# TensorE's waits on itself behind the borders of its instruction pieces: further back and more of them

## The chip, the cores and the metric

The kernel runs on one core of one Trainium2 chip. The metric is the device time of one launch in microseconds. Five engines of the core work side by side, each with its own instruction stream: TensorE (PE, with its weight loads PEld), VectorE (DVE), ScalarE (ACT), GpSimd (POOL) and SyncE (SP), which here issues the transfers. They wait for each other by semaphores.

## What is computed

The input x has 2048 tokens of 512 values. It is normalized, and an attention with a memory runs over it in 64 segments of 32 tokens; each segment's 8 memory rows come out of the segment before, so the segments form a chain. A two-layer network with gelu follows for all tokens.

```python
# A: for each of 64 segments, M = 8 memory rows, 32 heads of 128
h = concatenate([mem, xs]);  q, k, v = h @ Wq, h @ Wk, h @ Wv
p = softmax(mask(q k^T * 128**-0.5));  o = (p v) @ Wo
mem = o[:, :8];  outs.append(o[:, 8:])
# whole
h  = x + A(layernorm(x))
h2 = h + gelu(layernorm(layernorm(h)) @ w1 + b1) @ w2 + b2     # 512 -> 1792 -> 512
```

## The kernel before

All weights of the attention stay in SBUF (WQ, WK, WV, WO). A segment multiplies a pack hT of 32 columns (24 tokens and 8 memory rows) with WQ, WK and WV. A matmul with 32 stationary columns fills a quarter of the array, so four of them, on four column groups, run together: four matmuls of 512 columns are one *unit* of a projection. The remaining 8 tokens of each of four segments are gathered in a second pack, hB, and projected once per four segments; this work (called F in the program) fills places where TensorE would wait. Then come the scores of memory rows (SC0, SC1: L1122) and of tokens (SA: L1179), two softmaxes on VectorE, ScalarE and GpSimd, the products with v (PV0, PV1, PVA: L1153, L1157, L1225, L1231) and the output projection (WO: L1264, a run of 64 matmuls of 256 columns in eight units; L1303 for hB). L946 are matmuls that load their weights, L689 matmuls that reuse those that the array holds, L944 weight loads without a matmul. The last stage, behind some 710 us, is the two-layer network (L1660, L1667).

The program is recorded as a list of operations with estimated durations, and a scheduler (class `Sched`) writes each engine's stream from it. TensorE's order is fixed by hand; each operation gets a planned start, and from the planned order the scheduler works out which semaphore each operation must wait for. An operation signals its engine's semaphore on its last instruction only if somebody waits for it.

TensorE's stream is some 40,000 instructions. The program takes it to come in pieces of 256 instructions (`FETCH_N`). The method `pads` inserts harmless extra weight loads (L944) to move the borders of the pieces to chosen places, `windows` keeps transfers off the times of the borders, and `pauses` is the one that this change touches:

```python
for first in self.heads:                       # first unit behind each border
    n, i = 0, first
    while n < PAUSES and i < len(pe) and pe[i].at < pe[first].at + PAUSE_IN:
        o = pe[i]
        j = bisect.bisect_right(ends, o.start - PAUSE_US) - 1
        if not o.waits and 0 <= j < i:
            o.waits = [pe[j]]
            pe[j].sig = True
            n += 1
        i += 1
```

A unit close behind a border that waits for nothing else gets a wait on the last unit of TensorE itself that by plan ended at least `PAUSE_US` before it. TensorE executes in order, so such a wait orders nothing: it holds back the reading of instructions until the array has got so far. The numbers are at L31.

Of the kernel before, what the change touches and what calls it, by code (L numbers as in the profile page):

```python
# [27 lines left out]
LATE = dict(Q0=0.1, K0=0.1, Q1=-0.5, K1=-0.4, V0=2.0, SC0=2.0, SC1=1.6, V1=1.8, F=1.3, PV0=1.0, PVA=1.0, PV1=0.95, WO=0.4, F2=0.5, SA=0.5)  # L28
KEEP = True
WINDOWS, WIN_LO, WIN_HI, WIN_BEHIND = True, 1.0, -0.8, 0.4  # L30
PAUSES, PAUSE_IN, PAUSE_US = 3, 64, 0.5  # L31
KEPT, LEAD = 3, 9
REST = (0, 1, 4, 5, 6, 8, 9)
ORDER0 = (6, 7, 8, 9, 10, 11, 0, 1, 2, 3, 4, 5, 12, 13)
# [1746 lines left out]
```

## Time and profile before

| what | us |
|---|---|
| median of 3 runs | 805.2 (802.64 to 805.48) |
| the profiled execution, its time | 805.6 |
| its span, first to last instruction | 803.9 |
| TensorE busy | 770.4 |
| VectorE, ScalarE, GpSimd busy | 585.3, 529.2, 311.4 |
| the stage of the segments | about 60 to 700 |

A segment takes a little over 10 us there: the runs of L1264, one per segment, start at 223.18 and 233.81 us, for instance. The rows name a line, an engine, an operation and the tiles as out<-in; "x" is a count; "idle before" is the time that the engine stood still before it, with what ended it. A weight load has its own row (PEld) and runs beside matmuls. The ends of matmuls are modelled, so the steps from start to start tell more than the lengths.

### The profile page before, as it was taken

How to read it: one execution, taken by the hardware profiler on the slowest of the kernel's cores; microseconds unless marked ns; L12 is line 12 of the kernel's file. 1: busy time of each engine (PE TensorE's matmuls, PEld its weight loads, DVE VectorE, ACT ScalarE, POOL GpSimd, SP SyncE). 2: the span in 40 equal slices, each digit the busy share in tenths (PEclk: the TensorE clock that was granted, in tenths of full speed). 3: DMA queues.
4: the chain of work that ended last, by engine and by line, in shares of the span. 5: the costliest groups of instructions: out<-in, count | busy, mean ns of one | idle time of the engine just before them, and what ended most of it. 6: DMA issues, size and time to landing. Idle time of an engine off the chain costs nothing.

```text
span 803.9 us, 44855 instructions
## 1 busy us (share of the span) xinstructions
PE 770.4 (96%) x19573; PEld 423.6 (53%) x20093; DVE 585.3 (73%) x1865; ACT 529.2 (66%) x1381; POOL 311.4 (39%) x836
## 2 busy tenths in 40 slices
PE   4788999999999999999999999999999999999998
PEld 1345455555555555556665555556556564544443
DVE  3267888888888888888888888888888887833111
ACT  1446777767776777776767777777776777653342
POOL 3013223444343444444434444444453425276200
PEclk9989999999999999999999999999999999999999
DMA  8960000111201010103020201030112222266200
GB/s 337 393 194 11 3 21 20 24 38 23 37 15 46 10 50 10 44 11 57 4 52 8 52 9 50 11 50 4 50 31 62 45 58 53 62 184 157 53 27 26
DMA packets 65453, 48.11 MB, mean 60 GB/s; under 512 B 29028, under 2 KB 61676, under 8 KB 65260
## 3 DMA queue, kind: packets, MB, share of 16 engines
q1 hardware_dynamic: 64928, 44.98, 20.4%
q8 instruction: 156, 2.56, 1.4%
q14 instruction: 37, 0.30, 0.1%
q10 hardware_dynamic: 332, 0.27, 0.1%
HBM read 31.08 MB, written 8.13 MB: 49 GB/s over the span
## 4 chain that ended last, share of the span: by engine, by line
PE 91%; DMA 2%; DVE 2%; SPq 2%; issue 1%; ACT 1%; DVEq 0%
PE high L946 33%; PE high L689 17%; PE quad L1264 15%; PE quad L1667 6%; PE high L1660 5%; PE high L1303 3%; DMA WQ<-in_A_Wq_dram 2%; SPq L849 2%; PE quad L1122 2%; PE quad L1179 2%; PE quad L1225 2%; PE high L1459 2%; PE high L1153 1%; PE quad L1153 1%; PE high L1264 1%
## 5 line engine op out<-in xcount | busy, mean ns | idle before, releaser
L946 PE MATMUL high<-WQ,hT 128*32 128x512 bf16 x1796 | 158.2, 383 | 3.8 <-DVE hT L1270 3.0
L1202 POOL TENSOR_TENSOR PA<-SA,rsa 128x256 bf16<-128x256 f32 x64 | 39.6, 619 | 235.5 <-DVE rsa L1194 148.0
L689 PE MATMUL high<-WK,hT 128*32 128x512 bf16 x1260 | 127.3, 379 | 0.1
L1264 PE MATMUL quad<-WO,OT 128*32 128x256 bf16 x4032 | 122.7, 273 | 0.2 <-issue 0.2
L946 PE MATMUL high<-WV,hT 128*32 128x512 bf16 x1528 | 117.0, 381 | 0.0
L965 ACT ACTIVATE kq<-high 128x512 bf16<-128x512 f32 x160 | 94.2, 598 | 26.7 <-PE high L946 23.3
L964 ACT CAST kq<-high 128x512 bf16<-128x512 f32 x161 | 93.7, 582 | 21.4 <-PE high L946 19.6
L1264 PEld LDWEIGHTS quad<-WO,OT 128*32 128x32 bf16 x4032 | 101.9, 97 | 6.9 <-issue 1.7
L1210 POOL COPY BD<-PTA 32x128 f32<-32x128 f32 x256 | 79.6, 311 | 16.3 <-DVE PTA L1206 0.6
L946 PEld LDWEIGHTS high<-WQ,hT 128*32 128x32 bf16 x1796 | 52.8, 95 | 62.0 <-issue 28.9
L987 DVE STREAM_TRANSPOSE KALL<-kq 128x256 f32<-128x256 f32 x160 | 69.4, 434 | 10.9 <-ACT kq L964 8.1
L964 ACT CAST VS<-high 128x512 bf16<-128x512 f32 x126 | 73.1, 580 | 0.0
L944 PEld LDWEIGHTS <-hT 128*32 128x32 bf16 x3064 | 50.7, 96 | 32.7 <-DVE hT L1270 6.3
L1276 DVE STREAM_TRANSPOSE TT<-quad 128x256 f32<-128x256 f32 x63 | 28.3, 449 | 50.8 <-PE quad L1264 50.7
L1663 ACT ACTIVATE WQ<-high,b1t 128x512 bf16<-128x512 f32 x42 | 28.9, 687 | 51.9 <-PE high L1660 51.9
L964 ACT CAST OT<-quad 128x128 bf16<-128x128 f32 (+1 forms) x128 | 47.8, 375 | 21.8 <-PE quad L1157 21.5
L1021 ACT COPY KALL<-KALL 128x128 f32<-128x128 f32 x62 | 18.5, 298 | 59.0 <-PE quad L1179 58.8
L987 DVE STREAM_TRANSPOSE QT<-kq 128x256 f32<-128x256 f32 x128 | 54.8, 428 | 1.9 <-ACT kq L965 1.6
L946 PE MATMUL high<-WK,hT 128*32 128x512 bf16 x788 | 55.4, 379 | 0.0
L1122 PEld LDWEIGHTS quad<-KALL,ZC 128*32 128x32 bf16 x2016 | 32.3, 96 | 42.2 <-POOL BD L1210 18.1
L689 PE MATMUL high<-WV,hT 128*32 128x512 bf16 x520 | 54.5, 387 | 0.0
L1316 POOL TENSOR_TENSOR opT<-TTB,TTS 32x64 bf16<-32x64 f32 x128 | 40.0, 312 | 35.0 <-DVE opT L1270 18.6
(182 smaller groups left out, 1612.4 us busy)
## 6 DMA issues: line engine op xcount, KB each, us to landing
WV<-in_A_Wv_dram SPq DMA_DIRECT2D x4, 1024.0 KB, 10.5
WK<-in_A_Wk_dram SPq DMA_DIRECT2D x4, 1024.0 KB, 18.5
WQ<-in_A_Wq_dram SPq DMA_DIRECT2D x4, 1024.0 KB, 20.4
WO<-in_A_Wo_dram SPq DMA_DIRECT2D x16, 256.0 KB, 7.6
v_last<-VSB SPq DMA_DIRECT2D x60, 64.0 KB, 2.2
VBD<-v_last SPq DMA_DIRECT2D x60, 64.0 KB, 2.6
h_mid<-xr SPq DMA_DIRECT2D x16, 128.0 KB, 2.0
WQ<-h_mid SPq DMA_DIRECT2D x4, 512.0 KB, 4.2
```

What stands on the lines that cost most here:

```text
L689: return e.add_instruction(mybir.InstMatmult(name="I-%d" % (4000000 + _kept[0]), engine=mybir.EngineType.PE, start_tensor_calc=start, stop ...
L944: e.ldweights(l, tile_position=(0, 32 * j))
L946: ins = e.matmul(o, l, m, start=(k == 0), stop=(k == DC - 1), tile_position=(0, 32 * j), skip_group_check=True)
L964: return {"act": (lambda e: e.copy(out, src), t_act(n, ps_)), "dve": (lambda e: e.tensor_copy(out, src), 0.155 + 1.0e-3 * n * fast)}
L965: return {"act": (lambda e: e.mul(out, src, scale_), t_act(n, ps_)), "dve": (lambda e: e.tensor_scalar(out, src, scale_, None, ALU.mult), ...
L987: S.op("dve", lambda e: e.transpose(out, src), reads=[("kq", i)], writes=[key], dur=t_dve(256) + 0.02)
L1122: ins = e.matmul(o[32 * j:32 * j + 32, :], zc_window(h), rhs, start=False, stop=(i == 3), tile_position=(0, 32 * j), skip_group_check=True)
L1210: S.narrow(S.op("pool", lambda e, j=j, rows=rows: e.tensor_copy(words(BD[rows, par, :, j, :, :]), words(PTA[rows, 0:4])), reads=["PTA"], w ...
L1264: ins = e.matmul(ps[bank][32 * j:32 * j + 32, 0:256], lhs(slot(h)), wo_cols(h, b), start=(k == 0), stop=(k == 15), tile_position=(0, 32 * ...
L1316: return e.tensor_tensor(o[32 * q:32 * q + 32, c:c + 2], x, y, ALU.add)
L1660: ins = e.matmul(ps[bank][:, 0:SBT], W1[:, cc, fc * P:(fc + 1) * P], hnT_of(k)[:, cc, :], start=(cc == 0), stop=(cc == DC - 1))
L1667: S.op("pe", lambda e: e.matmul(quad[:, t, :], gT_of(k, fc)[:, t * P:(t + 1) * P], W2[:, fc, :], start=(fc == (0 if k else ORDER0[0])), st ...
```

## The change

Three numbers: up to ten units behind a border get a wait, where it was three; they may lie up to 192 instructions behind the border's first unit, where it was 64; and the unit waited for has by plan ended 0.9 us ago, where it was 0.5.

```diff
-PAUSES, PAUSE_IN, PAUSE_US = 3, 64, 0.5
+PAUSES, PAUSE_IN, PAUSE_US = 10, 192, 0.9
```

No operation is added, moved or taken away on any engine: only waits and signals of TensorE on itself. Of the 407 waits of TensorE on itself, all stay, 394 of them on another unit than before; there are 1343 now. The signals on TensorE rise from 1270 to 1936.

The first place, on TensorE: the piece that begins at about 221.4 us in the trace. Its first wait (L946, group at 221.81) stays and points two units further back, which the order doesn't show. Behind it come the products with v, and then the run of L1264; sem_act is ScalarE's semaphore, sem_pe TensorE's own. The piece's end is in the run of L1179 behind it.

```order
 L1157 MATMUL high<-PTC,VBD 128x64 x2
 L1264 MATMUL quad<-WO,OT 32x256 [waits sem_act]
-L1264 MATMUL quad<-WO,OT 32x256 x31
-L1264 MATMUL quad<-WO,OT 32x256 [waits sem_act]
-L1264 MATMUL quad<-WO,OT 32x256 x31
+L1264 MATMUL quad<-WO,OT 32x256 x7
+L1264 MATMUL quad<-WO,OT 32x256 [waits sem_pe]
+L1264 MATMUL quad<-WO,OT 32x256 x7
+L1264 MATMUL quad<-WO,OT 32x256 [waits sem_pe]
+L1264 MATMUL quad<-WO,OT 32x256 x7
+L1264 MATMUL quad<-WO,OT 32x256 [waits sem_pe]
+L1264 MATMUL quad<-WO,OT 32x256 x7
```

Nothing moved; five new waits stand in this run (three shown, two more behind the second wait on ScalarE), between waits on ScalarE that were there.

The second place, on TensorE: the end of such a run, then hB's output projection and the token scores of another segment (at about 163 us), where a piece has fewer waits on other engines.

```order
 L1264 MATMUL quad<-WO,OT 32x256 [waits sem_act]
-L1264 MATMUL quad<-WO,OT 32x256 x31
-L1303 MATMUL high<-WO,OTB 32x512 x8
+L1264 MATMUL quad<-WO,OT 32x256 x7
+L1264 MATMUL quad<-WO,OT 32x256 [waits sem_pe]
+L1264 MATMUL quad<-WO,OT 32x256 x7
+L1264 MATMUL quad<-WO,OT 32x256 [waits sem_pe]
+L1264 MATMUL quad<-WO,OT 32x256 x7
+L1264 MATMUL quad<-WO,OT 32x256 [waits sem_pe]
+L1264 MATMUL quad<-WO,OT 32x256 x7
+L1303 MATMUL high<-WO,OTB 32x512 [waits sem_pe]
+L1303 MATMUL high<-WO,OTB 32x512 x3
```

Here, too, only waits came in, one for each unit.

## The prediction

> **What bounds the kernel now.** I read the page's busy times and clock first, then the middle stage by windows, then TensorE's waits in it, then the chain. The page:
>
> ```profile
> span 803.9 us, 44855 instructions
> PE 770.4 (96%) x19573; PEld 423.6 (53%) x20093; DVE 585.3 (73%) x1865; ACT 529.2 (66%) x1381; POOL 311.4 (39%) x836
> PEclk9989999999999999999999999999999999999999
> q8 instruction: 156, 2.56, 1.4%
> PE 91%; DMA 2%; DVE 2%; SPq 2%; issue 1%; ACT 1%; DVEq 0%
> ```
>
> TensorE is busy for 96% at full clock and is 91% of the chain. The q8 line is how its program arrives: 156 packets, 2.56 MB, so 16 KB each; 19573 matmuls and 20093 weight loads over 156 packets are about 255 instructions a packet. These are the pieces of the change. The stage of the segments (columns: us, then busy us and count of PE, PEld, DVE, ACT, POOL, clock, DMA share, GB/s) and TensorE's own waits in it (total, times, longest):
>
> ```profile
> 60.00:640.00 580.00, 572.85 (x16648) 329.05 (x17272) 487.95 (x1595) 423.11 (x1152) 245.29 (x680) 1.00 0.13 29
> PE quad L1179 <- issue: 2.1, 8, 0.4
> PE high L946 <- DVE hT L1270: 2.0, 3, 0.8
> PE high L1153 <- DVE PTC L1139: 0.8, 2, 0.5
> PE high L946 <- issue: 0.7, 3, 0.4
> PE quad L1153 <- ACT EC L1131: 0.3, 1, 0.3
> PE high L1157 <- issue: 0.3, 2, 0.2
> PE quad L1264 <- issue: 0.2, 1, 0.2
> ```
>
> In 580 us TensorE lacks 7.15 us of being busy all the time. The largest part of its waits is "issue", time in which no semaphore was late: 2.1 + 0.7 + 0.3 + 0.2 = 3.3 us in 14 stops. None of TensorE's rows names TensorE as releaser. One of the stops, in order of time:
>
> ```profile
> 224.76 0.28 PE L1264 MATMUL quad<-WO,OT 128*32 128x256 bf16 x4
> 225.08 0.39 PE L689 MATMUL high<-WQ,hB 128*32 128x512 bf16 x4
> 225.30 0.21 PE L1179 MATMUL quad<-KALL,QT 128*32 128x40 bf16 x7
> 225.83 0.34 PE L1179 MATMUL quad<-KALL,QT 128*32 128x40 bf16 x25 [0.32 <-issue]
> ```
>
> A run of 32 equal matmuls stops after the seventh. In the program the first of the 32 is instruction 242 of its piece, and seven matmuls with their weight loads are 14 instructions: the stop is at instruction 256, on the border. So I read "issue" here as a piece that came late. The transfers of that time (40 slices of 0.1 us from 222 to 226):
>
> ```profile
> GB/s 0 0 0 0 0 0 0 0 0 164 0 0 0 0 0 0 0 0 0 0 0 0 0 0 0 0 0 0 0 0 0 0 0 0 0 0 0 0 0 0
> q8 instruction: 1, 0.02, 2.0%
> ```
>
> One packet, nothing beside it: it starts at 222.9 and takes 2.0% of 16 engines over 4 us, 1.28 us, so it lands near 224.2, and the starved matmul starts 1.6 us later. The border before it lies in the group that starts at 221.38 (next fence), so the packet started 1.5 us behind that border. A faster start of that packet is the only thing that the change could win.
>
> **What the change does, part by part.** The built program has the same 40058 TensorE instructions in the same order, and the other queues are unchanged, SP's and POOL's too. Waits of TensorE on itself rise from 407 to 1343 and its signals from 1270 to 1936.
>
> *The 407 waits that stay* point further back: in projections at the unit six back, where it was four. The place just behind that border:
>
> ```profile
> 221.38 0.40 PE L946 MATMUL high<-WQ,hB 128*32 128x512 bf16 x4
> 221.59 0.40 PE L689 MATMUL high<-WQ,hB 128*32 128x512 bf16 x4
> 221.60 0.12 PEld L946 LDWEIGHTS high<-WQ,hB 128*32 128x32 bf16 x4 [0.32 <-PE high L946]
> 221.81 0.40 PE L946 MATMUL high<-WQ,hB 128*32 128x512 bf16 x4
> 222.03 0.40 PE L689 MATMUL high<-WQ,hB 128*32 128x512 bf16 x4
> ```
>
> The weight load at 221.60 waited 0.32 us on TensorE's own work, and the matmuls go on every 0.215 us without a gap: today's waits cost nothing. Their spare time: the unit four back starts 4 x 0.215 = 0.86 ahead and lasts 0.40, and the weights load 0.21 ahead, which leaves 0.25 us. Six back it is 1.29 - 0.40 - 0.21 = 0.68 us. What is queued behind such a wait is TensorE's own stream alone; the other engines wait for matmuls, which don't move. Term: 0.
>
> *The 936 new waits* have the same 0.68 us of spare time. Bound from rows of the chain:
>
> ```profile
> 213.09 1.86 PE quad L1264 x64
> 223.18 1.86 PE quad L1264 x64
> 510.89 1.95 PE quad L1264 x64
> 582.35 2.00 PE quad L1264 x64
> 634.60 2.04 PE quad L1264 x64
> ```
>
> The run of 64 at 213.09 has three such waits in it, the one at 223.18 none; both take 1.86. With a resolution of 0.01 us that is at most 0.01/3 = 3.3 ns a wait, 3.1 us for 936. Below: no reason for a gain in itself. I take 0, since the two rows are equal, and keep 3.1 as the upper end. (The three rows over 1.86 are runs with a border in them: small stops.)
>
> *The 666 new signals.* The same two runs have one signal more in the one than in the other, so at most 10 ns each, 6.7 us for all, if each lay bare. They end a group whose followers are already streaming, and the steps above don't change; I take 0. The Trainium skill has a rule that speaks against the change: in "TensorE: Matmul & The Clock Gate", section "The cost: per-tile semaphore tail", each increment on a matmul's end adds 26.3 ns to the tail, since increments are written one after another. An estimate by that page is 666 x 26.3 ns = 17.5 us, if no tail were covered; the equal runs of 1.86 don't show it.
>
> *What goes away as a hold.* At 221.60 the hold of 0.32 us is shorter than the 0.43 us by which the wait moves back, so it vanishes, and the sequencer gets past that place up to 0.32 us sooner. If the next piece is asked for when the sequencer has got so far, the packet at 222.9 moves forward. But next in its way stand waits on VectorE and ScalarE for the group L1153, which the change leaves alone. What is at stake: 14 stops of 3.3 us by the waits view, each longer by the modelled length of the matmul ahead of it,
>
> ```profile
> L1179 PE MATMUL quad<-KALL,QT 128*32 128x40 bf16 x2016 | 27.4, 182 | 2.4 <-issue 2.1
> ```
>
> so 3.3 + 14 x 0.18 = 5.8 us, and with small stops like 2.04 - 1.86 = 0.18 in the rows above about 7 us. That is the whole prize. Ends: -7 and 0 by this; I take a tenth, -0.7 us, nearest to no gain, since the VectorE wait takes the hold over.
>
> *What stands longer.* Up to ten waits reach to instruction 192 of a piece, where three reached to 64. They keep the sequencer within 0.68 us plus a weight load of the array over much of a piece, where it could run further ahead. A piece entered later asks for its successor later. In the run of L1264 (the first of the two places in the section on the change) the new waits stand between two waits on ScalarE that are there anyway, and near the next border there are again such waits. Term: 0, with an upper end of 0.3 us a stop, 14 x 0.3 = 4.2 us.
>
> The Trainium skill, "Runtime: NRT & Kernel Launch", section "Instruction fetch mechanics", says that programs stream in 16 KiB blocks of 256 instructions and that a border's cost is mostly hidden. The trace agrees with the size (16 KB, 255) and not quite with the rest: 14 of some 140 borders in this stage stop TensorE. By that rule the prize would be 0 and the time 805.2.
>
> **Sum.** 0 + 0 + 0 - 0.7 + 0 = -0.7 us against the profiled execution's 805.6 (span 803.9 and 1.7 around it): 804.9. That execution is 0.4 above the median 805.2, so the median comes to 804.5 us.
>
> **Rivals.**
>
> *Pieces come sooner.* The vanished hold (0.32 at 221.60) starts the packet sooner at most starved borders: 14 x 0.3 = 4.2 us, 801.0; at most 7, 798.2. For it: the hold stands right behind the border of the piece whose successor was late. Against: the waits on VectorE and ScalarE close behind.
>
> *Pieces come later* (the other side). The longer hold puts the sequencer 0.3 us later over the borders; the 14 starved pieces lose 14 x 0.3 = 4.2 us, 809.4, and pieces that now come just in time join them. It decides from about 0.3 us a piece on. For it: two rows show stops of 0.4 us already, so there is no reserve. Against: 64 units of L1264 take 1.86 us, with or without waits.
>
> *Signals cost.* 10 ns each, bare: +6.7, 811.9; a third of it would be 807.4. Against: the equal steps of 0.215 us.
>
> *Nothing changes at all.* The waits are all long satisfied and the packets start as before: 805.2. This and my forecast can't be told apart by time.
>
> **Chances.** The likeliest (804.5) and "nothing changes" together 0.70; pieces sooner 0.16; pieces later 0.10; signals 0.04. A change is told from none by about 0.5%, 4.0 us. So faster 0.17 (the sooner rival and a little of the spread of 802.64 to 805.48 in the runs), slower 0.12 (the later rival and the dearer half of the signals), same 0.71. The range for 8 in 10 reaches down to the sooner rival's 4.2 us, 801.0, and up to 804.5 + 3.1 (the bound of the waits), 807.6; outside lie about 0.08 below and 0.10 above.
>
> **What would show it.** If I am right: TensorE's waits on "issue" in this stage again 2 to 5 us in 10 to 20 stops, on borders; runs of L1264 at 1.86 us with five more waits in them; the projection step still 0.215 us; weight loads that wait on PE shorter than 0.32 each, though there are more of them. The sooner rival: issue rows nearly gone, packets of q8 earlier behind their borders. The later rival: more stops, longer, at the same places. Signals: runs of L1264 longer than 1.86 everywhere, by 0.01 or more a signal. I am wrong if the request of a piece depends on something the waits do to the sequencer that this trace can't show, since 0.2 us on each packet is worth about 3 us.

## The result and the profile after

The changed kernel takes 822.74 us (median of 4 runs, 820.94 to 826.45) against 803.99 us (4 runs, 802.64 to 805.48) for the kernel before, measured beside it: 1.0247 times as long, 95% interval 1.0223 to 1.027. It is slower by about 19 us, where I had forecast 804.5 us. The profiled execution took 824.03 us, 18.4 more than the 805.6 of before, and its span is longer by the same 18.4. Its page:

```profile
span 822.3 us, 44855 instructions
PE 773.9 (94%) x19573; PEld 424.5 (52%) x20093; DVE 586.2 (71%) x1865; ACT 530.1 (64%) x1381; POOL 314.1 (38%) x836
q8 instruction: 156, 2.56, 1.3%
PE 90%; issue 3%; DMA 2%; DVE 2%; SPq 2%; ACT 1%; DVEq 0%
L1264 PE MATMUL quad<-WO,OT 128*32 128x256 bf16 x4032 | 125.7, 273 | 13.8 <-issue 12.3
```

The number of instructions and of packets is that of before, and the busy times rise by a few us at most. What grew is "issue" in the chain, from 1% to 3% of the span, and it sits at one line: the matmuls of L1264 had 13.8 us of idle time ahead of them. The stage of the segments, and TensorE's waits in it, in the views that the prediction used:

```profile
60.00:640.00 580.00, 560.42 (x16170) 320.33 (x16786) 476.35 (x1553) 412.19 (x1122) 239.91 (x659) 1.00 0.13 28
PE quad L1264 <- issue: 11.6, 14, 1.2
PE high L946 <- DVE hT L1270: 2.3, 3, 0.8
PE quad L1179 <- issue: 2.0, 6, 0.7
PE quad L1264 <- PE quad L1264: 1.5, 2, 0.9
PE high L1153 <- DVE PTC L1139: 1.2, 3, 0.5
PE high L946 <- PE high L689: 0.7, 2, 0.5
PE high L1157 <- issue: 0.2, 1, 0.2
```

In the same 580 us TensorE now gets through 16170 matmuls, where it was 16648; for the work of before it would need 580 x (16648/16170 - 1) = 17.1 us more, so nearly all of the 18.4 us is lost here. The row of L1264 grew from 0.2 us in one stop to 11.6 in 14, and two more stops (1.5 us, where the matmul behind the border happens to carry one of the new waits) carry TensorE's own name. That is 13.1 - 0.2 = 12.9 us in 16 stops; with the modelled 0.27 us of the matmul ahead of each, 17.2 us. The rest of the stage is as it was: the clock is 1.00, the waits on VectorE differ by less than 1 us, and the 0.7 us of L946 behind L689 are border stops too, which before stood as 0.7 us of L946 on issue.

One stop, beside the same place of the kernel before. First before: the second scores' weight loads, the V projection ahead of them, the run of L1264, and the transfers from 394 to 398 us (40 slices of 0.1 us, then the one packet in them):

```profile
394.52 0.40 PE L689 MATMUL high<-WV,hT 128*32 128x512 bf16 x4
395.92 0.21 PEld L1122 LDWEIGHTS quad<-KALL,ZC 128*32 128x32 bf16 x16 [0.30 <-POOL BD L1210]
398.24 1.93 PE L1264 MATMUL quad<-WO,OT 128*32 128x256 bf16 x64
GB/s 0 0 0 0 0 0 0 0 0 0 0 0 0 0 0 0 164 0 0 0 0 0 0 0 0 0 0 0 0 0 0 0 0 0 0 0 0 0 0 0
q8 instruction: 1, 0.02, 1.8%
```

After, the same rows, and the transfers from 403 to 407 us:

```profile
403.48 0.40 PE L689 MATMUL high<-WV,hT 128*32 128x512 bf16 x4
404.88 0.21 PEld L1122 LDWEIGHTS quad<-KALL,ZC 128*32 128x32 bf16 x16 [0.29 <-POOL BD L1210]
407.21 0.40 PE L1264 MATMUL quad<-WO,OT 128*32 128x256 bf16 x6
408.23 1.03 PE L1264 MATMUL quad<-WO,OT 128*32 128x256 bf16 x29 [0.63 <-issue]
GB/s 0 0 0 0 0 0 0 0 0 0 0 0 0 0 0 0 0 0 0 0 0 0 0 0 0 0 0 164 0 0 0 0 0 0 0 0 0 0 0 0
q8 instruction: 1, 0.02, 1.5%
```

The array's work is the same to 0.01 us: from the V matmuls to the second scores 1.40 us in both, to the run of L1264 3.72 and 3.73. The packet is not: before it starts in the slice at 395.6, 0.3 us ahead of the second scores; after, in the slice at 405.7, 0.8 us behind them. It is 1.1 us later against the same work, with no other transfer in the window in either kernel, and the run of L1264 stops at its border until the piece is there. The time went into pieces whose packets started later.

Of the 133 borders from segment 5 to segment 60, read packet by packet from both traces, 18 have this shape: the border lies in the K projection shortly ahead of the scores, and the piece ends in or just ahead of the run of L1264. In these 18 the packet starts 1.55 us behind its border on average before, 2.60 us after. In no other kind that occurs ten times or more does the mean move by more than 0.1 us.

### The profile page after: what moved, and what is told of

It is laid out like the page before. It is cut to its first block, busy times and chain, and to the rows that moved or that the text cites. A ratio compares the mean times of both kernels' runs of the same rounds, so it can differ in the third digit from the quotient of the medians.

```text
span 822.3 us, 44855 instructions
## 1 busy us (share of the span) xinstructions
PE 773.9 (94%) x19573; PEld 424.5 (52%) x20093; DVE 586.2 (71%) x1865; ACT 530.1 (64%) x1381; POOL 314.1 (38%) x836
## 4 chain that ended last, share of the span: by engine, by line
PE 90%; issue 3%; DMA 2%; DVE 2%; SPq 2%; ACT 1%; DVEq 0%
PE high L946 32%; PE high L689 17%; PE quad L1264 15%; PE quad L1667 6%; PE high L1660 4%; PE high L1303 3%; DMA WQ<-in_A_Wq_dram 2%; SPq L849 2%; PE quad L1179 2%; PE quad L1122 2%; PE quad L1225 2%; PE high L1459 2%; PE high L1153 1%; PE quad L1153 1%; PE high L1264 1%
## 5 line engine op out<-in xcount | busy, mean ns | idle before, releaser
L946 PE MATMUL high<-WQ,hT 128*32 128x512 bf16 x1796 | 158.1, 383 | 4.3 <-DVE hT L1270 3.3
L1264 PE MATMUL quad<-WO,OT 128*32 128x256 bf16 x4032 | 125.7, 273 | 13.8 <-issue 12.3
L689 PE MATMUL high<-WK,hT 128*32 128x512 bf16 x1260 | 127.3, 379 | 0.0
L946 PE MATMUL high<-WV,hT 128*32 128x512 bf16 x1528 | 115.8, 379 | 0.0
L1264 PEld LDWEIGHTS quad<-WO,OT 128*32 128x32 bf16 x4032 | 101.9, 97 | 23.1 <-issue 16.4
L946 PEld LDWEIGHTS high<-WQ,hT 128*32 128x32 bf16 x1796 | 52.4, 95 | 60.7 <-issue 22.8
L946 PE MATMUL high<-WK,hT 128*32 128x512 bf16 x788 | 56.9, 389 | 0.0
L689 PE MATMUL high<-WV,hT 128*32 128x512 bf16 x520 | 53.1, 379 | 0.0
```

Of the source, the lines that this page charges most:

```text
L689: return e.add_instruction(mybir.InstMatmult(name="I-%d" % (4000000 + _kept[0]), engine=mybir.EngineType.PE, start_tensor_calc=start, stop ...
L946: ins = e.matmul(o, l, m, start=(k == 0), stop=(k == DC - 1), tile_position=(0, 32 * j), skip_group_check=True)
L1264: ins = e.matmul(ps[bank][32 * j:32 * j + 32, 0:256], lhs(slot(h)), wo_cols(h, b), start=(k == 0), stop=(k == 15), tile_position=(0, 32 * ...
```

## Experiments

The waits on TensorE itself have three numbers: how many behind a border, how far they reach, and how long ago the unit waited for ended. The first four runs take them apart; the kernel before, measured beside them, took 801.8 us (15 runs). "Hold" is the theory that the shorter distance held the reading where it did good, "reach" that the waits far into a piece do the harm, "signals and waits" that their number costs.

**Distance alone.**

```diff
-PAUSES, PAUSE_IN, PAUSE_US = 10, 192, 0.9
+PAUSES, PAUSE_IN, PAUSE_US = 3, 64, 0.9
```

> Three waits within 64 instructions as before, but on work planned to have ended 0.9 us ago; 407 waits, 1336 signals. Theory hold (the looser waits no longer hold TensorE's instruction reading in a short stretch behind a border, and the next piece is asked for later in the pieces that end in the run of L1264): about 17 us over before, stops of about 1 us on borders inside the runs of L1264. Theory reach (many waits far behind the border keep the reading back): as before, within 3 us. Theory signals and waits (each wait or signal costs): as before, at most 66 x 26 ns = 2 us over.

Measured: 817.19 us, 1.0177 (1.0147 to 1.0206). The waits of the stage have

```profile
PE quad L1264 <- issue: 11.6, 16, 1.1
```

The distance by itself makes most of the loss, 15.4 of 19 us: the same 407 waits as before, nearly all of them looser.

**Number and reach alone.**

```diff
-PAUSES, PAUSE_IN, PAUSE_US = 10, 192, 0.9
+PAUSES, PAUSE_IN, PAUSE_US = 10, 192, 0.5
```

> Ten waits within 192 instructions as in the changed kernel, but on work planned to have ended 0.5 us ago; 1343 waits, 1812 signals. Theory hold: as before, within 3 us. Theory reach: about 17 us over before or more, since these waits hold harder. Theory signals and waits: 542 more signals of 26 ns, about 14 us over before.

Measured: 801.42 us, 0.9995 (0.9978 to 1.0013). It has 936 more waits and 542 more signals than the kernel before, and L1264 has no row among the waits; the issue rows are

```profile
PE quad L1179 <- issue: 1.3, 4, 0.6
PE high L1303 <- issue: 0.4, 1, 0.4
```

"Reach" and "signals and waits" fall: ten waits to instruction 192 cost nothing if they are near ones.

**No pauses at all.**

```diff
-PAUSES, PAUSE_IN, PAUSE_US = 10, 192, 0.9
+PAUSES, PAUSE_IN, PAUSE_US = 0, 64, 0.5
```

> No waits of TensorE on itself; 1114 signals. Theory hold: at least 17 us over before, with the same stops in the runs of L1264 and perhaps more at other borders. Theory reach: as before or faster. Theory signals and waits: up to 4 us faster than before.

Measured: 819.07 us, 1.02 (1.0162 to 1.0239), with

```profile
PE quad L1264 <- issue: 13.9, 17, 1.2
```

Without any of these waits the loss is 17.3 us, about that of the changed kernel. So the loose waits do no harm; they fail to do a good that the near ones did.

**Near waits only behind the 26 borders in the K projection ahead of the scores**, everything else as changed:

```diff
-j = bisect.bisect_right(ends, o.start - PAUSE_US) - 1
+j = bisect.bisect_right(ends, o.start - (0.5 if (pe[first - 1].tag or (0, ''))[1] == 'K1' else PAUSE_US)) - 1
```

> The changed kernel, but behind the 26 borders that lie in a K1 unit (their pieces end mostly in a run of L1264) the waits are on work planned to have ended 0.5 us ago, as before; 1343 waits, 1896 signals. Theory hold: as before, within 3 us, though all but 40 of the new signals are there. Theory reach and theory signals and waits: about 17 us over before, as the changed kernel.

Measured: 802.6 us, 1.002 (0.9999 to 1.0041); L1264 has no row among the waits. The good is done in these pieces, and nowhere else to any size.

What is special about them? In the built program no matmul and no weight load carries more than one wait: where a unit waits for two engines, the first wait goes into an instruction of its own ahead of the unit, a *separate wait*. The program puts 386 of them into TensorE's stream. In the pieces in question one stands in front of the first scores, 5 to 22 instructions behind the border, and one in front of the second scores, some 70 to 90 behind it; the near waits lie mostly between the two. The traces also record these instructions, and "that separate wait" is from here on the one in front of the second scores. In the 18 pieces the next packet starts, without pauses, 0.89 to 1.58 us behind that separate wait in 17 and 0.35 ahead of it in one; in the changed kernel 0.90 to 1.65 us behind it in 16 and up to 0.36 ahead in two; in the kernel before from 1.13 ahead of it to 0.37 behind in all 18. None lies between 0.37 and 0.89. From this came the theory "separate wait": while the reading stands in a separate wait, the next piece isn't asked for; the packet then comes about 0.9 us after that wait is over. Its rival "held early" says that only being held is what counts.

**No pauses, and no separate waits in the segments.** Each of 295 first waits rides on a spare weight load (of a tile that is there anyway) which takes the place of the separate instruction, so no border moves:

```diff
 for p in o.waits:
     ...
         e.wait_ge(sems[p.eng], p.sigcount)
+    if engname == "pe" and len(o.waits) == 2 and p is o.waits[0] and ... and o.tag[1] in INLOAD:
+        e.ldweights(self.spare, tile_position=(0, 0))
 ins = o.fn(e)
```

> No waits of TensorE on itself, as in the run without them. Besides, in the segments each of the 295 separate wait instructions in front of a TensorE operation with two waits is replaced by a spare weight load that carries the wait; the count of instructions and the borders stay. Theory separate wait (while TensorE's sequencer sits in a wait instruction of its own it does not ask for the next piece; a wait that a weight load carries leaves it free): the packets behind borders in K1 start about 1.5 us behind them again and the time is that of before within 4 us. Theory held early (the sequencer must be held by a wait shortly behind the border, of whatever kind what follows): packets about 2.7 us behind, about 17 us over before, as without waits.

Measured: 814.0 us, 1.015 (1.0097 to 1.0203; the kernel before 801.79). The time alone would speak against "separate wait"; the waits speak for it. In the stage they read, whole (lines are two further down than in the kernel before, here and in the runs with waits on loads below),

```profile
PE high L948 <- DVE hT L1272: 1.7, 3, 0.8
PE high L1155 <- DVE PTC L1141: 0.8, 2, 0.5
PE quad L1181 <- issue: 0.4, 1, 0.4
PE quad L1155 <- DVE PTC L1141: 0.3, 1, 0.3
```

One border stop of 0.4 us is left, and in the 18 pieces the packet starts 0.10 us behind the border on average, without any pause. The time went to spare loads themselves, as two of them show in order of time (the next runs test it):

```profile
402.36 0.19 PE L1159 MATMUL quad<-PTC,VBD 64*128 64x64 bf16 x2
402.48 0.09 PEld L610 LDWEIGHTS <-ident 128*32 128x32 bf16 x1
402.59 0.41 PE L1227 MATMUL quad<-BD,VS 64*128 64x64 bf16 x16
402.84 0.22 PE L1233 MATMUL quad<-BDL,VBD 64*128 64x64 bf16 x4
402.99 0.09 PEld L610 LDWEIGHTS <-ident 128*32 128x32 bf16 x1
403.09 0.26 PE L1155 MATMUL high<-PTC,VS 64*128 64x16 bf16 x8
```

**The same with the pauses of before** (3, 64, 0.5).

> The kernel before with the 295 separate wait instructions replaced by spare weight loads that carry the wait. Theory separate wait: as before or up to 6 us faster, since the packets behind borders in F units, now 1.7 us behind, start sooner too and the stops in the runs of L1179 go. Theory held early: as before within 2 us.

Measured: 813.46 us, 1.0143 (1.0088 to 1.0198), no wait on issue in the stage. Both theories missed the time, since neither counted what the loads cost (below). With the separate waits gone, near pauses and none give the same time, where they differed by 17 us.

**A distance between the two.**

```diff
-PAUSES, PAUSE_IN, PAUSE_US = 10, 192, 0.9
+PAUSES, PAUSE_IN, PAUSE_US = 3, 64, 0.7
```

> Three waits within 64 instructions as before, on work planned to have ended 0.7 us ago: one unit further back than before, one nearer than in the changed kernel. Theory held early and theory separate wait alike: the hold ends 0.2 us sooner, and part of the 18 packets comes late: 4 to 14 us over before. If the time is that of before or that of the far waits (17 over), the hold works as a step and not by its length.

Measured: 812.37 us, 1.0129 (1.0049 to 1.021), with

```profile
PE quad L1264 <- issue: 10.0, 12, 1.2
```

Piece by piece it is one or the other, nothing between: in 7 of the 18 the packet starts at least 0.14 us ahead of the separate wait, in 11 it starts 0.90 to 1.56 us behind it.

**One near wait behind each border.**

```diff
-PAUSES, PAUSE_IN, PAUSE_US = 10, 192, 0.9
+PAUSES, PAUSE_IN, PAUSE_US = 1, 64, 0.5
```

> One wait within 64 instructions behind each border (148 waits), on work planned to have ended 0.5 us ago. If it is the hold shortly before the next wait instruction that counts (the second and third wait), about 17 us over before; if any hold behind the border will do, as before within 3 us.

Measured: 819.33 us, 1.0216 (1.0157 to 1.0275), with

```profile
PE quad L1264 <- issue: 13.6, 16, 1.4
```

One near wait is as good as none. This fits a hold that must last until close ahead of the separate wait, but no run moved one near wait there by itself.

**Waits on loads where that is free.** The next three leave alone the 124 separate waits at the two places just shown, where the loads cost time: in front of L1225 and in front of the second L1153, which follows L1231 (L1227, L1155 and L1233 in those kernels). First without pauses: 171 waits, 124 in front of the scores of memory rows and 47 in front of the first products with v (L1153). The expectations of this run and the next name other lines besides; in front of L1231, L1179 and L1264 stands none of the 295.

```diff
-INLOAD = ('SC0', 'SC1', 'PV0', 'PV1', 'PVA', 'SA', 'WO')
+INLOAD = ('SC0', 'SC1', 'PV0', 'SA', 'WO')
```

> No pause at all, and of the second waits of a unit only those in front of the scores (L1122, L1179), the first products with v (L1157) and the output projection (L1264) ride on a spare weight load, 171 of them; the 124 in front of L1225 and L1231 stay separate instructions. Theory 'separate wait': with no separate wait in front of the scores the pieces that begin in a K unit are asked for at once, so the stops in L1264 (13.9 us without pauses) are gone as they were with all 295; and the 0.345 us a segment that the loads cost in front of L1225 and L1231 (63 segments, 21.7 us) are not paid: 814.0 - 21.7 = 792 us, at most 797, faster than the kernel before. Rival 'loads cost everywhere': the 14 us that all 295 loads cost beyond the removed stops spread evenly over them, 171 of 295 then cost 12 to 13 us: about 805 us. Theory 'held early' (a pause is needed to be early): stops return, about 815 us.

Measured: 797.83 us against 802.19, 0.9951 (0.9935 to 0.9967). The stops are gone and it is faster than the kernel before, but it stays over 5 us above the 792 expected, and just above the limit of 797. At the place shown above it has

```profile
395.02 0.19 PE L1159 MATMUL quad<-PTC,VBD 64*128 64x64 bf16 x2
395.05 0.40 PE L1227 MATMUL quad<-BD,VS 64*128 64x64 bf16 x16
395.29 0.22 PE L1233 MATMUL quad<-BDL,VBD 64*128 64x64 bf16 x4
395.43 0.26 PE L1155 MATMUL high<-PTC,VS 64*128 64x16 bf16 x8
```

The steps are 0.03 and 0.14 us, where the loads made them 0.23 and 0.25. The 124 loads fewer are worth 814.0 - 797.83 = 16.2 us, 0.13 each, less than the 21.7 I had expected; where the other 5 us lie I can't say.

**Only the 124 waits in front of the scores of memory rows.**

```diff
-INLOAD = ('SC0', 'SC1', 'PV0', 'SA', 'WO')
+INLOAD = ('SC0', 'SC1')
```

> No pause, and only the 124 second waits in front of the scores of memory rows (L1122) ride on a spare weight load. Theory 'separate wait': in a piece that begins in a K unit the reading stands at the separate wait in front of L1122 when it should ask, so these 124 alone take most of the stops in L1264 away: 792 to 803 us, and at most 3 us of waits on issue in L1264. Rival: another separate wait of the piece (in front of L1225, L1231 or L1264) is the one that counts; then the stops stay at 10 us or more and the time at 812 to 819 us.

Measured: 798.36 us, 0.9958 (0.9939 to 0.9977). The waits on issue that are left:

```profile
PE quad L1181 <- issue: 0.7, 2, 0.4
PE high L948 <- issue: 0.6, 2, 0.3
```

These 124 alone take all stops in L1264 away: 819.07 to 798.36 with no pause in either.

**The changed kernel's numbers (10, 192, 0.9) with the 171 waits on loads.**

> The changed kernel (ten units, 192 instructions, 0.9 us) with the same 171 waits on spare loads. Theory 'separate wait': the loose waits hurt only because the reading then runs into a separate wait; with those gone they cost nothing, so the time is that of the same edit without pauses within 3 us, 792 to 798 us. Rival 'the distance itself makes the request late': the stops in L1264 stay near 11 us and the time is 808 to 815 us.

Measured: 797.46 us, 0.9945 (0.9927 to 0.9963), equal to the run without pauses. At the place shown at the start (here the transfers from 389.8 to 393.8 us):

```profile
390.40 0.40 PE L691 MATMUL high<-WV,hT 128*32 128x512 bf16 x4
391.75 0.24 PEld L1124 LDWEIGHTS quad<-KALL,ZC 128*32 128x32 bf16 x16
394.12 1.93 PE L1266 MATMUL quad<-WO,OT 128*32 128x256 bf16 x64
GB/s 0 0 0 0 0 164 0 0 0 0 0 0 0 0 0 0 0 0 0 0 0 0 0 0 0 0 0 0 0 0 0 0 0 0 0 0 0 0 0 0
q8 instruction: 1, 0.02, 1.6%
```

The packet starts in the slice at 390.3, 1.4 us ahead of the second scores, and the run of L1264 is whole again. The loose waits that cost 19 us cost nothing here.

**The load beside the separate wait.** One rival was left: that the load paces the reading, whatever carries the wait. Here the same 124 loads stand idle in front of the separate waits, without pauses (the padding counts them too, which the cut leaves out):

```diff
 for o in self.streams[engname]:
+    if engname == "pe" and extra(o):      # the same 124 units
+        e.ldweights(self.spare, tile_position=(0, 0))
     for p in o.waits:
```

> No pause; the same 124 spare weight loads in front of the scores of memory rows (L1122) as in the run that moved the waits onto them, but here each stands idle in front of the separate wait, which stays (the padding shrinks by about as much, and some borders lie elsewhere). Theory 'separate wait': it is the wait's form that keeps the next piece from being asked for, so the stops come back: 812 to 825 us, with 8 us or more of waits on issue in the stage of the segments. Rival 'the load itself' (a load at that place paces the reading, whatever carries the wait): as with the waits on the loads, 797 to 802 us and under 3 us of such waits.

Measured: 817.77 us against 803.74, 1.0182 (1.0122 to 1.0243), with (lines three further down)

```profile
PE quad L1267 <- issue: 12.0, 15, 1.6
```

The borders lie in other segments here, but 22 of them have the shape of the 18, and in 15 of these the packet starts 0.89 to 1.75 us behind the separate wait. The load does nothing; it is the form of the wait.

## Why the prediction was wrong

**The step that failed** is "What goes away as a hold", and it failed twice. It read the 0.32 us of idle time ahead of the weight load at 221.60 as a hold that the looser wait would end. Here is that load after the change, and then with no pause at all:

```profile
226.20 0.12 PEld L946 LDWEIGHTS high<-WQ,hB 128*32 128x32 bf16 x4 [0.31 <-PE high L946]
223.39 0.12 PEld L946 LDWEIGHTS high<-WQ,hB 128*32 128x32 bf16 x4 [0.31 <-issue]
```

The 0.31 or 0.32 us stand there with the near wait, with the loose one and with none, since loads of 0.12 us come every 0.43 us. So they measured no hold, and none vanished. The packet starts 1.6 us behind that border before and after: at the place quoted the change did not move it.

The step then let the packet only move forward ("the packet at 222.9 moves forward") and gave the term -7 to 0 us, -0.7 taken. The quoted piece is not among the 18 that count. In those the packet moved back by 1.05 us on average: in 16 of them it starts only 0.90 to 1.65 us behind the end of the separate wait, where it started at most 0.37 us behind it before. The term was +17 to +18 us. What the near waits did there, to get the next piece asked for before the reading came to the separate wait, is nowhere in the prediction; no row of before bore out its condition "If the next piece is asked for when the sequencer has got so far".

**The rival "Pieces come later"** had the sign, the place (borders that starve) and "pieces that now come just in time join them": 14 stops became some 24. Its reason was wrong: it blamed waits that hold longer and reach further, which cost nothing by themselves (801.42), and priced a piece at 0.3 us where it is about 1. I had made the waits' looseness a gain; it was the loss, and their number cost nothing.

**The 936 new waits at 0:** right. The run of L1264 at the first place, 1.86 us before with none of these waits in it, has five now:

```profile
227.79 1.86 PE quad L1264 x64
```

In the chain's rows 43 such runs of 1.86 us are left whole, 54 before.

**The 407 waits at 0** was right only for what a wait costs by itself. "What is queued behind such a wait is TensorE's own stream alone" left out the request of the next piece: the same 407 waits, looser, made 15.4 us of the loss.

**The 666 signals at 0:** right. By the Trainium skill, "TensorE: Matmul & The Clock Gate", section "The cost: per-tile semaphore tail", an estimate for 542 more is 542 x 26.3 ns = 14.3 us, if no tail were covered; the run with 542 more took 801.42 against 801.8 us. That fits tails covered by the matmuls behind them.

**The prize of "Pieces come sooner", at most 7 us:** about right in size, in another kernel: with the scores' waits on loads the stops vanish and 4.4 to 4.7 us are won (797.46 to 797.83 against 802.19).

**The rule of the Trainium skill** on pieces ("Runtime: NRT & Kernel Launch", section "Instruction fetch mechanics": a border's cost is mostly hidden) holds in the kernels without separate waits in front of the scores, where at most 1.3 us of waits on issue were left, and fails by 17 us in the changed one.

**The prediction's own sign of being wrong** named it: a request that "depends on something the waits do to the sequencer" and that the trace of before can't show. I gave the later side 0.10 all the same, because I priced only the ways that I could see in rows.

**What stays open:** why a sequencer that stands in a separate wait doesn't ask for the next piece, and where exactly the asking happens. No trace records where the reading stands or when a piece is asked for; that the packet follows the request by about 0.9 us is read from the gap alone. The waits in front of the first and of the second scores were moved onto loads together, so no run tells how much each counts. The other separate waits may delay packets too: with all 295 on loads the packets behind borders of the other kinds start 0.5 to 0.8 us sooner than in the run without pauses, but those pieces had time to spare.

## What to carry to other kernels

A wait that orders nothing may still be doing work: before loosening or removing it, run the kernel without it once and look at what starts earlier or later, packets of instructions included. When a pause helps for a reason that the trace doesn't show, look for what the pause keeps the sequencer out of; here it was a wait in an instruction of its own, and putting that wait on an instruction that goes to the array made the pauses needless and beat them by 0.5%. A gain of that kind should be priced in place: the same spare load was free in one phase and cost 0.13 us in another.

## What was not expected of the hardware

- In this kernel a separate wait on TensorE's queue delays the packet with the next 16 KB of program: in the 18 pieces it starts 0.9 us or more behind the end of such a wait, or ahead of it to 0.4 us behind, and not in between. Waits carried by weight loads don't do this (mean start behind the border 0.10 us against 2.73 in the 18 pieces, both without pauses).
- A spare weight load of 128 rows and 32 columns among matmuls on tiles of 64 rows and 128 columns lengthens the step from 0.03 to 0.23 us and from 0.14 to 0.25; the 124 among matmuls on tiles of 128 rows and 32 columns showed no loss (1.0182 times the kernel before with them idle, 1.02 without them, both without pauses).
- 936 waits of TensorE on itself and 542 signals cost less than the measurement can tell (0.9978 to 1.0013).
